# The first input loads of a fused residual + norm kernel split into small fp32 tiles

## The chip, the core and the metric

The kernel runs on one core of a Trainium2 chip. The core has five engines with a queue of instructions each: TensorE (PE, with its weight loads shown as PEld), VectorE (DVE), ScalarE (ACT), GpSimd (POOL) and SyncE (SP), and 16 DMA engines that they share. Every engine takes its instructions in order. The metric is the device time of one execution in microseconds (us), less is better.

## What is computed

```python
B, S, D = 4, 256, 256
x       = randn(B, S, D)          # float32, 1024 rows of 256
w_block = randn(D, D) * 0.05      # float32
gamma   = abs(randn(D)) + 0.5     # float32

h = maximum(x @ w_block, 0.0)
y = x + h
mu = y.mean(-1, keepdims=True)
sigma = sqrt(y.var(-1, keepdims=True) + 1e-6)
out = ((y - mu) / sigma * gamma).astype(float32)
```

The matmul is small (1024 x 256 by 256 x 256); x and the output are 1 MB each in HBM, w is 256 KB.

## The kernel before

The 1024 rows are cut into two halves (h = 0, 1) of 128 partitions x 4 rows (f), so a partition holds 4 consecutive rows of x. Each half is loaded by one DMA from POOL's queue that casts fp32 to bf16 on the way (L74); the tiles are called `x_sb_97` and `x_sb_99` in the trace. The weights w and gamma are loaded as fp32 from ACT's queue (L56, L61) and cast to bf16 on ACT (w, L58) and on DVE (gamma, L63). POOL also builds the identity matrix for the transposes (masks.py:197, a memset, and masks.py:199, an affine select).

The work then runs over four pairs of rows, `pr` = 0 to 3, each 128 partitions x 2 rows x 256:

1. PE transposes the pair in four 128x128 pieces into PSUM (L84), ACT copies them to SBUF (`xt_sb`, L89).
2. PE multiplies: four matmuls, two per row, that add up over the two halves of D (`ph`, L94).
3. ACT takes the relu out of PSUM (`relu_h`, L103). DVE adds x (`y`, L106), takes mean and variance per row (bn_stats L113, bn_aggr L114), ACT the square root (`std`, L117), DVE the reciprocal (`rstd`, L119), and DVE subtracts the mean and multiplies (`tq`, L123, two per pair).
4. POOL multiplies by gamma and writes fp32 (`o`, L133), SP issues the store (L137).

Square root needs another function table than the first copies, so ACT loads a table (ACT_TABLE_LOAD) ahead of its first `std`.

A scheduler (the Tile framework) sets the order of the instructions on each engine at build time and puts in the semaphore waits. The order in the program text is its starting point, not what stands on the engines.

Of the kernel before, what the change touches and what calls it, by code (L numbers as in the profile page):

```python
# [1 line left out]

# [15 lines left out]
def kernel(
    ctx: ExitStack,  # L20
    tc: tile.TileContext,
    x: bass.AP,
    w_block: bass.AP,
    gamma: bass.AP,
    out: bass.AP,
):
    nc = tc.nc
    P = 128

    x_flat = x.flatten_outer_dims()  # L30
    out_flat = out.flatten_outer_dims()
    N, D = x_flat.shape
    assert D == 256 and N == 1024
    KC = D // P
    G = 4
    NH = N // (P * G)
    PAIR = 2
    n_pairs = N // (P * PAIR)
# [24 lines left out]
    nc.vector.tensor_copy(out=gamma_sb, in_=gamma_stage)  # L63

    eps_sb = const.tile([P, 1], FP32)
    nc.vector.memset(eps_sb, eps)

    ident = const.tile([P, P], BF16)
    make_identity(nc, ident)

    x_sb = []
    for h in range(NH):
        t_ = xp.tile([P, G, D], BF16, name=f"x_sb{h}", tag=f"x{h}")
        nc.gpsimd.dma_start(out=t_, in_=x_v[h])  # L74
        x_sb.append(t_)

    for pr in range(n_pairs):
        h = (pr * PAIR) // G
        f0 = (pr * PAIR) % G

        pxt = ps_xt.tile([P, PAIR, KC, P], BF16)
        for t in range(PAIR):
            for c in range(KC):
                nc.tensor.transpose(  # L84
                    pxt[:, t, c, :], x_sb[h][:, f0 + t, ts(c, P)], ident
                )

        xt_sb = xtp.tile([P, PAIR, KC, P], BF16)
        nc.scalar.copy(out=xt_sb, in_=pxt)  # L89

        ph = ps_h.tile([P, PAIR, D], FP32)
        for t in range(PAIR):
# [23 lines left out]
        std = stat.tile([P, PAIR], FP32)
        nc.scalar.activation(out=std, in_=mv[:, :, 1], func=AF.Sqrt, bias=eps_sb)  # L117
        rstd = stat.tile([P, PAIR], FP32)
        nc.vector.reciprocal(out=rstd, in_=std)  # L119

        tq = op_.tile([P, PAIR, D], BF16)
        for t in range(PAIR):
# [9 lines left out]
        o = op_.tile([P, PAIR, D], FP32, tag="out")
        nc.gpsimd.tensor_tensor(  # L133
            out=o, in0=tq, in1=gamma_sb.to_broadcast([P, PAIR, D]), op=ALU.mult
        )
# [32 lines left out]
```

## Time and profile before

| | us |
|---|---|
| median of 6 runs | 26.32 (26.08 to 26.65) |
| the profiled execution's own time | 26.32 |
| its span (first to last instruction) | 24.5 |

| engine | busy us (share of the span) |
|---|---|
| DVE | 9.4 (38%) |
| ACT | 8.5 (34%) |
| POOL | 6.6 (27%) |
| PE | 5.5 (22%) |

No engine is busy for half of the span, so the sum of busy time tells little. What counts is the chain of work that ends last, followed back from the end: it holds DVE for 26% of the span, DMA for 24% (the load of `x_sb_97`), ACT for 15% and PE for 10%. The profile's other views used below are the timeline of each engine, the waits, the DMA queues, and the windows, which give the busy time in chosen stretches.

### The profile page before, as it was taken

How to read it: one execution, taken by the hardware profiler on the slowest of the kernel's cores; microseconds unless marked ns; L12 is line 12 of the kernel's file. 1: busy time of each engine (PE TensorE's matmuls, PEld its weight loads, DVE VectorE, ACT ScalarE, POOL GpSimd, SP SyncE). 2: the span in 40 equal slices, each digit the busy share in tenths (PEclk: the TensorE clock that was granted, in tenths of full speed). 3: DMA queues.
4: the chain of work that ended last, by engine and by line, in shares of the span. 5: the costliest groups of instructions: out<-in, count | busy, mean ns of one | idle time of the engine just before them, and what ended most of it. 6: DMA issues, size and time to landing. Idle time of an engine off the chain costs nothing.

```text
span 24.5 us, 182 instructions
## 1 busy us (share of the span) xinstructions
PE 5.5 (22%) x32; PEld 3.8 (15%) x32; DVE 9.4 (38%) x34; ACT 8.5 (34%) x15; POOL 6.6 (27%) x12
## 2 busy tenths in 40 slices
PE   0000000000039599994994000000000000000000
PEld 0000000000038277772770000000000000000000
DVE  0000000004000000599930999999998991000000
ACT  0029836000003945599999990000242000000000
POOL 3398600000000000000000049509802966920000
PEclk9999999999999999999999999975555555555555
DMA  0009727699973000000000000009107400913700
GB/s 0 0 7 245 264 32 72 122 160 204 197 137 57 0 0 0 0 0 0 0 0 0 0 0 0 0 0 377 50 0 280 147 0 0 381 47 127 301 0 0
DMA packets 1280, 1.97 MB, mean 80 GB/s; under 512 B 128, under 2 KB 512, under 8 KB 1280
## 3 DMA queue, kind: packets, MB, share of 16 engines
q0 software_dynamic: 288, 0.52, 13.0%
q1 hardware_dynamic: 576, 1.05, 11.4%
q10 hardware_dynamic: 416, 0.39, 5.6%
HBM read 1.44 MB, written 1.05 MB: 101 GB/s over the span
## 4 chain that ended last, share of the span: by engine, by line
DVE 26%; DMA 24%; ACT 15%; PE 10%; issue 5%; POOLq 5%; POOL 1%; DVEq 0%
DMA x_sb_97<-in_x_dram 24%; DVE tq L123 11%; PE ph L94 8%; ACT xt_sb L89 6%; DVE y L106 6%; ACT L117 5%; POOLq L163 5%; DVE bn_181 L113 3%; PE pxt L84 3%; DVE bn_213 L113 3%; ACT relu_h L103 2%; DVE rstd L119 2%; DVE mv L114 2%; ACT std L117 1%; POOL ident masks.py:197 1%
## 5 line engine op out<-in xcount | busy, mean ns | idle before, releaser
L133 POOL TENSOR_TENSOR o<-tq,gamma_sb 128x512 f32<-128x512 bf16 x4 | 4.7, 1173 | 14.1 <-DVE tq L123 12.5
L94 PE MATMUL ph<-w_sb,xt_sb 128*128 128x256 bf16 x16 | 3.6, 402 | 0.6 <-ACT xt_sb L89 0.6
L89 ACT COPY xt_sb<-pxt 128x512 bf16<-128x512 bf16 x4 | 2.1, 590 | 3.7 <-PE pxt L84 3.7
L123 DVE TENSOR_SCALAR tq<-y,mv,rstd 128x256 bf16<-128x256 bf16 x8 | 3.1, 434 | 0.1
L84 PE MATMUL pxt<-ident,x_sb_97 128*128 128x128 bf16 x8 | 1.0, 311 | 7.1 <-DMA x_sb_97<-in_x_dram 7.1
L103 ACT ACTIVATE relu_h<-ph 128x512 bf16<-128x512 f32 x4 | 2.3, 590 | 0.9 <-PE ph L94 0.9
L106 DVE TENSOR_TENSOR y<-x_sb_97,relu_h 128x512 bf16<-128x512 bf16 x2 | 0.8, 409 | 4.1 <-ACT relu_h L103 4.1
L94 PEld LDWEIGHTS <-xt_sb 128*128 128x128 bf16 x16 | 2.1, 140 | 1.8 <-ACT xt_sb L89 1.1
L117 ACT ACTIVATE std<-mv,eps_sb 128x2 f32<-128x2 f32 x4 | 1.2, 295 | 3.3 <-DVE mv L114 3.3
L63 DVE CAST gamma_sb<-gamma_stage 128x256 bf16<-128x256 f32 x1 | 0.3, 294 | 4.9 <-DMA gamma_stage<-in_gamma_dram 4.9
L58 ACT ACT_TABLE_LOAD x1 | 1.3, 1283 | 1.7 <-PEq L152 1.7
L84 PEld LDWEIGHTS <-x_sb_97 128*128 128x128 bf16 x8 | 0.8, 140 | 7.1 <-DMA x_sb_97<-in_x_dram 7.1
L106 DVE TENSOR_TENSOR y<-x_sb_99,relu_h 128x512 bf16<-128x512 bf16 x2 | 1.6, 802 | 0.0
L117 ACT ACT_TABLE_LOAD x1 | 1.3, 1283 | 0.0
L84 PE MATMUL pxt<-ident,x_sb_99 128*128 128x128 bf16 x8 | 1.1, 314 | 0.0
L119 DVE RECIPROCAL rstd<-std 128x2 f32<-128x2 f32 x4 | 0.7, 164 | 1.1 <-ACT std L117 1.0
L84 PEld LDWEIGHTS <-x_sb_99 128*128 128x128 bf16 x8 | 0.9, 151 | 0.1
L74 POOL DMA_DIRECT2D x_sb_97<-in_x_dram x1 | 0.7, 714 | 0.3 <-issue 0.3
L58 ACT CAST w_sb<-w_stage 128x512 bf16<-128x512 f32 x1 | 0.6, 617 | 0.5 <-DMA w_stage<-in_w_block_dram 0.5
L113 DVE BATCH_NORM_STATS2 bn_213<-y 128x6 f32<-128x256 bf16 x2 | 0.8, 384 | 0.0
L113 DVE BATCH_NORM_STATS2 bn_117<-y 128x6 f32<-128x256 bf16 x2 | 0.8, 418 | 0.0
L113 DVE BATCH_NORM_STATS2 bn_149<-y 128x6 f32<-128x256 bf16 x2 | 0.8, 418 | 0.0
(13 smaller groups left out, 3.5 us busy)
## 6 DMA issues: line engine op xcount, KB each, us to landing
out_dram<-o SPq DMA_DIRECT2D x4, 256.0 KB, 2.0
w_stage<-in_w_block_dram ACTq DMA_DIRECT2D x1, 256.0 KB, 2.7
x_sb_97<-in_x_dram POOLq DMA_DIRECT2D x1, 256.0 KB, 5.8
x_sb_99<-in_x_dram POOLq DMA_DIRECT2D x1, 256.0 KB, 6.0
gamma_stage<-in_gamma_dram ACTq DMA_DIRECT2D x1, 128.0 KB, 4.5
```

The source lines that it names most:

```text
L58: nc.scalar.copy(out=w_sb, in_=w_stage)
L84: nc.tensor.transpose(pxt[:, t, c, :], x_sb[h][:, f0 + t, ts(c, P)], ident)
L89: nc.scalar.copy(out=xt_sb, in_=pxt)
L94: nc.tensor.matmul(ph[:, t, :], lhsT=xt_sb[:, t, c, :], rhs=w_sb[:, c, :], start=(c == 0), stop=(c == KC - 1),)
L103: nc.scalar.activation(out=relu_h, in_=ph, func=AF.Relu)
L106: nc.vector.tensor_tensor(out=y, in0=x_sb[h][:, f0 : f0 + PAIR, :], in1=relu_h, op=ALU.add)
L113: nc.vector.bn_stats(out=bn6[:, t, :], in_=y[:, t, :])
L117: nc.scalar.activation(out=std, in_=mv[:, :, 1], func=AF.Sqrt, bias=eps_sb)
L119: nc.vector.reciprocal(out=rstd, in_=std)
L123: nc.vector.tensor_scalar(tq[:, t, :], in0=y[:, t, :], scalar1=mv[:, t, 0:1], scalar2=rstd[:, t : t + 1], op0=ALU.subtract, op1=ALU.mult,)
L133: nc.gpsimd.tensor_tensor(out=o, in0=tq, in1=gamma_sb.to_broadcast([P, PAIR, D]), op=ALU.mult)
L163: with _tile.TileContext(nc) as tc:
```

## The change

- Of the first half of x, the first two rows per partition come as two tiles of 128 x 256 in **fp32**, `x_t0` and `x_t1`, loaded without a cast by SP. The other two rows are a bf16 tile `x_p1` (128 x 512) and the second half is a bf16 tile `x_p23` (128 x 1024); both are loaded with the cast by POOL, as before.
- w and gamma move from ACT's queue to SP's, behind the two x tiles; the cast of w moves from ACT to DVE.
- There are two identities, fp32 and bf16, both built ahead of POOL's loads.
- The work runs over five units in place of four pairs: u0 and u1 of one row per partition, u2, u3 and u4 of two. The transposes of u0 and u1 are in fp32.
- For u4 the multiplication by gamma moves from POOL to DVE, with a bf16 result `ob`, and its store moves to POOL's queue, which casts bf16 to fp32 on the way out.
- The pool of `y` has 4 buffers in place of 3; x tiles have one each.

```diff
+    ident_f32 = const.tile([P, P], FP32)
+    make_identity(nc, ident_f32)
+    ident = const.tile([P, P], BF16)
+    make_identity(nc, ident)
+
+    x_t0 = xp.tile([P, 1, D], FP32, name="x_t0", tag="x_t0")
+    nc.sync.dma_start(out=x_t0, in_=x_v[0][:, 0:1, :])
+    x_t1 = xp.tile([P, 1, D], FP32, name="x_t1", tag="x_t1")
+    nc.sync.dma_start(out=x_t1, in_=x_v[0][:, 1:2, :])
     w_stage = const.tile([P, KC, D], FP32)
-    nc.scalar.dma_start(out=w_stage, in_=w_block.rearrange("(kc p) n -> p kc n", p=P))
+    nc.sync.dma_start(out=w_stage, in_=w_block.rearrange("(kc p) n -> p kc n", p=P))
+    gamma_stage = const.tile([P, 1, D], FP32)
+    nc.sync.dma_start(out=gamma_stage, in_=gamma.partition_broadcast(P))
+    x_p1 = xp.tile([P, 2, D], BF16, name="x_p1", tag="x_p1")
+    nc.gpsimd.dma_start(out=x_p1, in_=x_v[0][:, 2:4, :])
+    x_p23 = xp.tile([P, G, D], BF16, name="x_p23", tag="x_p23")
+    nc.gpsimd.dma_start(out=x_p23, in_=x_v[1])
+
     w_sb = const.tile([P, KC, D], BF16)
-    nc.scalar.copy(out=w_sb, in_=w_stage)
+    nc.vector.tensor_copy(out=w_sb, in_=w_stage)
...
-    x_sb = []
-    for h in range(NH):
-        t_ = xp.tile([P, G, D], BF16, name=f"x_sb{h}", tag=f"x{h}")
-        nc.gpsimd.dma_start(out=t_, in_=x_v[h])
-        x_sb.append(t_)
+        idm = ident_f32 if x_dt == FP32 else ident
+        pxt = ps_xt.tile([P, 2, KC, P], x_dt, tag=f"pxt_{x_dt}")
+        for t in range(nt):
+            for c in range(KC):
+                nc.tensor.transpose(pxt[:, t, c, :], xs[:, t, ts(c, P)], idm)
...
+        if apply2_eng == "gp":
+            o = op_.tile([P, 2, D], FP32, tag="out_f32")
+            nc.gpsimd.tensor_tensor(
...
+            nc.sync.dma_start(out=out_v[h][:, f0 : f0 + nt, :], in_=o[:, 0:nt])
+        else:
+            ob = op_.tile([P, 2, D], BF16, tag="out_bf16")
+            nc.vector.tensor_tensor(
...
+            nc.gpsimd.dma_start(out=out_v[h][:, f0 : f0 + nt, :], in_=ob[:, 0:nt])
 
-        nc.sync.dma_start(out=out_v[h][:, f0 : f0 + PAIR, :], in_=o)
+    process_unit(x_t0, 0, 0, 1, "gp", "u0")
+    process_unit(x_t1, 0, 1, 1, "gp", "u1")
+    process_unit(x_p1, 0, 2, 2, "gp", "u2")
+    process_unit(x_p23[:, 0:2, :], 1, 0, 2, "gp", "u3")
+    process_unit(x_p23[:, 2:4, :], 1, 2, 2, "ve", "u4")
```

Three places show what the scheduler makes of it. On PE, at the start of the changed kernel (`x_t_92` and `x_t_94` are the fp32 tiles x_t0 and x_t1, `x_p_100` is x_p1, `x_p_102` is x_p23; the matmuls on `xt_sb` are first the two of u0, then the two of u1):

```order
L84 MATMUL pxt<-ident_f_82,x_t_92 128x128 x2
L84 MATMUL pxt<-ident_f_82,x_t_94 128x128 x2
L84 LDWEIGHTS x_p_100
L84 MATMUL pxt<-ident,x_p_100 128x128
L92 LDWEIGHTS xt_sb
L92 MATMUL ph<-w_sb,xt_sb 128x256
L92 LDWEIGHTS xt_sb
L92 MATMUL ph<-w_sb,xt_sb 128x256
```

The first transpose of u2, with its weight load from `x_p_100`, stands ahead of the first matmul of u0.

On ACT, the whole of the changed kernel's queue up to its end (128x256 are u0 and u1, the first two 128x512 copies are u2 and u3):

```order
L87 ACT_TABLE_LOAD
L87 CAST xt_sb<-pxt 128x256 x2
L101 ACTIVATE relu_h<-ph 128x256 x2
L87 COPY xt_sb<-pxt 128x512 x2
L101 ACTIVATE relu_h<-ph 128x512
L115 ACT_TABLE_LOAD
L115 ACTIVATE std<-mv,eps_sb 128x1 x2
L101 ACTIVATE relu_h<-ph 128x512
L87 COPY xt_sb<-pxt 128x512
L101 ACTIVATE relu_h<-ph 128x512
L115 ACTIVATE std<-mv,eps_sb 128x2 x3
```

The square roots of u0 and u1 stand behind the copies of u2 and u3, the relu of u2 and the table load.

On POOL, from the identities on, the changed kernel has:

```order
masks.py:197 MEMSET ident_f_82 128x128
masks.py:197 MEMSET ident 128x128
masks.py:199 ISA
masks.py:199 AFFINE_SELECT ident_f_82<-ident_f_82 128x128
masks.py:199 AFFINE_SELECT ident<-ident 128x128
L66 DMA x_p_100<-in_x_dram 128x512
L68 DMA x_p_102<-in_x_dram 128x1024
L134 TENSOR_TENSOR o<-tq,gamma_sb 128x256 x2
L134 TENSOR_TENSOR o<-tq,gamma_sb 128x512 x2
L149 DMA out_dram<-ob 128x512
```

Two memsets and two selects stand ahead of the first load, where before it was one memset, and the last store is now at the end of this queue.

## Rows read from the trace of the kernel before

**Rows 1.** The chain that ended last: start us, us, what.
```profile
1.25 5.83 DMA x_sb_97<-in_x_dram
...
11.92 1.28 ACT L117
13.21 0.30 ACT std L117
...
20.45 1.18 POOLq L163
```

**Rows 2.** The waits: total us, times, longest us.
```profile
PE pxt L84 <- DMA x_sb_97<-in_x_dram: 7.1, 1, 7.1
```

**Rows 3.** The timeline of POOL at the start: start us, us, instruction.
```profile
0.74 0.20 POOL masks.py:197 MEMSET ident<- 128x128 bf16 x1 [0.29 <-POOLq L152]
1.25 0.71 POOL L74 DMA_DIRECT2D x_sb_97<-in_x_dram  x1 [0.31 <-issue]
2.06 0.30 POOL masks.py:199 TENSOR_SCALAR_AFFINE_SELECT ident<-ident 128x128 bf16<-128x128 bf16 x1
2.30 0.56 POOL L74 DMA_DIRECT2D x_sb_99<-in_x_dram  x1
```

**Rows 4.** The timeline of ACT and DVE: the load of w, the cast of gamma.
```profile
0.74 0.42 ACTq L56 DMA_DIRECT2D w_stage<-in_w_block_dram  x1
...
5.76 0.29 DVE L63 CAST gamma_sb<-gamma_stage 128x256 bf16<-128x256 f32 x1 [4.89 <-DMA gamma_stage<-in_gamma_dram]
```

**Rows 5.** DMA issues: queue, count, KB each, median us from issue to landing.
```profile
out_dram<-o SPq DMA_DIRECT2D x4, 256.0 KB, 2.0
w_stage<-in_w_block_dram ACTq DMA_DIRECT2D x1, 256.0 KB, 2.7
x_sb_97<-in_x_dram POOLq DMA_DIRECT2D x1, 256.0 KB, 5.8
x_sb_99<-in_x_dram POOLq DMA_DIRECT2D x1, 256.0 KB, 6.0
gamma_stage<-in_gamma_dram ACTq DMA_DIRECT2D x1, 128.0 KB, 4.5
```

**Rows 6.** DMA queues, 3.4 to 3.7 us: packets, MB, share of 16 engines.
```profile
q0 software_dynamic: 1, 0.00, 17.0%
```

**Rows 7.** DMA queues, 5.0 to 5.5 us (q10: w and gamma).
```profile
q10 hardware_dynamic: 7, 0.00, 6.0%
```

**Rows 8.** DMA queues, 5.5 to 6.0 us (q0: POOL's loads of x).
```profile
q0 software_dynamic: 56, 0.11, 113.5%
```

**Rows 9.** Windows: stretch, its length, busy per engine, clock, DMA share, GB/s.
```profile
23.20:23.50 0.30, 0.00 (x0) 0.00 (x0) 0.00 (x0) 0.00 (x0) 0.00 (x0) 0.50 0.03 7
```

**Rows 10.** Timeline of PE: start us, us for the group, instruction.
```profile
7.12 1.03 PE L84 MATMUL pxt<-ident,x_sb_97 128*128 128x128 bf16 x8 [7.12 <-DMA x_sb_97<-in_x_dram]
8.41 1.89 PE L94 MATMUL ph<-w_sb,xt_sb 128*128 128x256 bf16 x8 [0.25 <-ACT xt_sb L89]
```

**Rows 11.** Groups of instructions: count, busy us, mean ns, idle before.
```profile
L103 ACT ACTIVATE relu_h<-ph 128x512 bf16<-128x512 f32 x4 | 2.3, 590 | 0.9 <-PE ph L94 0.9
L106 DVE TENSOR_TENSOR y<-x_sb_97,relu_h 128x512 bf16<-128x512 bf16 x2 | 0.8, 409 | 4.1 <-ACT relu_h L103 4.1
L119 DVE RECIPROCAL rstd<-std 128x2 f32<-128x2 f32 x4 | 0.7, 164 | 1.1 <-ACT std L117 1.0
```

**Rows 12.** Timeline of DVE and POOL, from 13.7 us on.
```profile
13.77 0.58 DVE L123 TENSOR_SCALAR tq<-y,mv,rstd 128x256 bf16<-128x256 bf16 x2
16.40 0.74 DVE L113 BATCH_NORM_STATS2 bn_181<-y 128x6 f32<-128x256 bf16 x2
17.06 0.16 DVE L114 BATCH_NORM_AGGREGATE mv<-bn_181 128x2 f32<-128x6 f32 x1
18.85 1.15 POOL L133 TENSOR_TENSOR o<-tq,gamma_sb 128x512 f32<-128x512 bf16 x1 [1.15 <-DVE rstd L119]
18.96 1.38 DVE L123 TENSOR_SCALAR tq<-y,mv,rstd 128x256 bf16<-128x256 bf16 x2
```

More of the change, by code (lines that the diff above doesn't have):

```diff
@@ L35 @@
     G = 4
-    NH = N // (P * G)
-    PAIR = 2
-    n_pairs = N // (P * PAIR)
     eps = 1e-6
@@ L45 @@
     const = ctx.enter_context(tc.tile_pool(name="const", bufs=1))
-    xp = ctx.enter_context(tc.tile_pool(name="xp", bufs=2))
+    xp = ctx.enter_context(tc.tile_pool(name="xp", bufs=1))
     xtp = ctx.enter_context(tc.tile_pool(name="xtp", bufs=3))
     hp = ctx.enter_context(tc.tile_pool(name="hp", bufs=3))
-    yp = ctx.enter_context(tc.tile_pool(name="yp", bufs=3))
+    yp = ctx.enter_context(tc.tile_pool(name="yp", bufs=4))
     op_ = ctx.enter_context(tc.tile_pool(name="op", bufs=3))
@@ L53 @@
     ps_h = ctx.enter_context(tc.tile_pool(name="ps_h", bufs=4, space=bass.MemoryType.PSUM))
-    w_stage = const.tile([P, KC, D], FP32)
-    nc.scalar.dma_start(out=w_stage, in_=w_block.rearrange("(kc p) n -> p kc n", p=P))
+    ident_f32 = const.tile([P, P], FP32)
[6 more added lines that the diff above has]
+    nc.sync.dma_start(out=x_t1, in_=x_v[0][:, 1:2, :])
+    w_stage = const.tile([P, KC, D], FP32)
+    nc.sync.dma_start(out=w_stage, in_=w_block.rearrange("(kc p) n -> p kc n", p=P))
[5 more added lines that the diff above has]
+    nc.gpsimd.dma_start(out=x_p23, in_=x_v[1])
     w_sb = const.tile([P, KC, D], BF16)
-    nc.scalar.copy(out=w_sb, in_=w_stage)
-    gamma_stage = const.tile([P, 1, D], FP32)
-    nc.scalar.dma_start(out=gamma_stage, in_=gamma.partition_broadcast(P))
+    nc.vector.tensor_copy(out=w_sb, in_=w_stage)
     gamma_sb = const.tile([P, 1, D], BF16)
@@ L66, with process_unit @@
     nc.vector.memset(eps_sb, eps)
-    ident = const.tile([P, P], BF16)
-    make_identity(nc, ident)
-    x_sb = []
-    for h in range(NH):
-        t_ = xp.tile([P, G, D], BF16, name=f"x_sb{h}", tag=f"x{h}")
-        nc.gpsimd.dma_start(out=t_, in_=x_v[h])
-        x_sb.append(t_)
[L77 to L82, printed above, removed]
-            for c in range(KC):
[L84 to L92, printed above, removed]
+    def process_unit(xs, h, f0, nt, apply2_eng, tagsfx):
+        x_dt = xs.dtype
+        idm = ident_f32 if x_dt == FP32 else ident
+        pxt = ps_xt.tile([P, 2, KC, P], x_dt, tag=f"pxt_{x_dt}")
+        for t in range(nt):
+            for c in range(KC):
+                nc.tensor.transpose(pxt[:, t, c, :], xs[:, t, ts(c, P)], idm)
+        xt_sb = xtp.tile([P, 2, KC, P], BF16)
+        nc.scalar.copy(out=xt_sb[:, 0:nt], in_=pxt[:, 0:nt])
+        ph = ps_h.tile([P, 2, D], FP32)
+        for t in range(nt):
             for c in range(KC):
@@ L100 @@
                 )
-        relu_h = hp.tile([P, PAIR, D], BF16)
-        nc.scalar.activation(out=relu_h, in_=ph, func=AF.Relu)
-        y = yp.tile([P, PAIR, D], BF16)
+        relu_h = hp.tile([P, 2, D], BF16)
+        nc.scalar.activation(out=relu_h[:, 0:nt], in_=ph[:, 0:nt], func=AF.Relu)
+        y = yp.tile([P, 2, D], BF16)
         nc.vector.tensor_tensor(
-            out=y, in0=x_sb[h][:, f0 : f0 + PAIR, :], in1=relu_h, op=ALU.add
+            out=y[:, 0:nt], in0=xs[:, 0:nt], in1=relu_h[:, 0:nt], op=ALU.add
         )
-        bn6 = stat.tile([P, PAIR, 6], FP32)
-        mv = stat.tile([P, PAIR, 2], FP32)
-        for t in range(PAIR):
+        bn6 = stat.tile([P, 2, 6], FP32)
+        mv = stat.tile([P, 2, 2], FP32)
+        for t in range(nt):
             nc.vector.bn_stats(out=bn6[:, t, :], in_=y[:, t, :])
             nc.vector.bn_aggr(out=mv[:, t, :], in_=bn6[:, t, :])
[L116 to L122, printed above, removed]
+        std = stat.tile([P, 2], FP32)
+        nc.scalar.activation(
+            out=std[:, 0:nt], in_=mv[:, 0:nt, 1], func=AF.Sqrt, bias=eps_sb
+        )
+        rstd = stat.tile([P, 2], FP32)
+        nc.vector.reciprocal(out=rstd[:, 0:nt], in_=std[:, 0:nt])
+        tq = op_.tile([P, 2, D], BF16)
+        for t in range(nt):
             nc.vector.tensor_scalar(
@@ L130 @@
             )
[L132 to L135, printed above, removed]
-        nc.sync.dma_start(out=out_v[h][:, f0 : f0 + PAIR, :], in_=o)
+        if apply2_eng == "gp":
+            o = op_.tile([P, 2, D], FP32, tag="out_f32")
+            nc.gpsimd.tensor_tensor(
+                out=o[:, 0:nt],
+                in0=tq[:, 0:nt],
+                in1=gamma_sb.to_broadcast([P, nt, D]),
+                op=ALU.mult,
+            )
+            nc.sync.dma_start(out=out_v[h][:, f0 : f0 + nt, :], in_=o[:, 0:nt])
+        else:
+            ob = op_.tile([P, 2, D], BF16, tag="out_bf16")
+            nc.vector.tensor_tensor(
+                out=ob[:, 0:nt],
+                in0=tq[:, 0:nt],
+                in1=gamma_sb.to_broadcast([P, nt, D]),
+                op=ALU.mult,
+            )
+            nc.gpsimd.dma_start(out=out_v[h][:, f0 : f0 + nt, :], in_=ob[:, 0:nt])
[4 more added lines that the diff above has]
+    process_unit(x_p23[:, 2:4, :], 1, 2, 2, "ve", "u4")
 _INS = ['x', 'w_block', 'gamma']
```

## Prediction, made before the changed kernel ran

> **What bounds the kernel now.** I read the chain of waits first, then the waits, then the timelines. The chain opens with the cast load of the first half of x: issued by POOL at 1.25, landed 5.83 later [rows 1], and until then PE stands idle for 7.1 us, its one long wait [rows 2]. From there one thread runs through transposes, copies, matmuls and relu, ACT's table load (11.92 to 13.20) and the first square root [rows 1], then DVE without a gap, then POOL's last multiplication by gamma (20.45 to about 21.65) and the last store, 2.0 from issue to landing [rows 1, 5]. The windows show that the store's data are through at about 23.2 [rows 9], so its landing is about 21.7 + 2.0 = 23.7; the span ends at 24.5, 0.8 after it. The profiled execution took 26.32 with a span of 24.5, so 1.8 lie outside the span; 26.32 is also the median. All sums below are spans, with 1.8 added at the end.
>
> So three stretches can shrink: the 7.1 at the start, the middle from the landing to DVE's end (7.1 to 20.3), and the 4.2 from DVE's end to the end.
>
> **The change, part by part.**
>
> *When the new first tiles land.* SP issues x_t0 at about 0.74, where ACT issued w [rows 4]. It has 128 KB and no cast; 256 KB took 2.0 for a store and 2.7 for w [rows 5], so it lands at 2.7 to 3.5, and x_t1 one issue (0.42) [rows 4] later. w is issued third, at about 0.74 + 2 x 0.42 = 1.6, and lands at 4.3, or 0.5 later if it shares the engines; its cast on DVE is bounded by twice the 0.29 of gamma's, which is half its size [rows 4], so w_sb is there by 5.4. The fp32 transposes have no row. A bf16 one takes 1.03 / 8 = 0.13 in a stream of eight [rows 10], which bounds it from below; four of them fit between 3.5 and the landing of x_p1 (6.3, below) even at 0.7 each, so I cost them at nothing; that cover is gone if one takes over 0.7. The same holds for ACT's two casts.
>
> *What that buys: nothing directly.* PE's order has the first transpose of u2 ahead of the first matmul of u0. PE takes its queue in order, so every matmul waits for x_p1, a cast load by POOL like the one that PE waits for today. The early tiles only shorten what comes behind that load.
>
> *When x_p1 lands.* Before, the first load was issued at 1.25. Now a second memset (0.20) and two selects (0.30 each) stand ahead of it [rows 3]: 1.25 + 0.8 = 2.05, and x_p23 0.75 later, at 2.8. From issue to landing there are two bounds. From above the old 5.8 [rows 5]: 7.85. From below, the queue without disturbance: 0.71 of issue [rows 3], 0.9 to the end of a first packet (an estimate, half of the 1.7 between the issue's end, 1.96, and the first packet of this queue, which ended by 3.7 [rows 6], behind w), 8 packets per engine of half the bytes at half of 16 x 0.5 x 1.135 / 56 = 0.16 [rows 8], 0.65, and 0.5 from the last data to the landing, as at the store's end (23.2 to 23.7): 2.8, so 4.85. In between: x's queue reaches its full rate only as gamma's packets end, at about 5.5 [rows 7, 8], and gamma is now issued 0.8 later, behind more bytes, so it is again in the way; but x_p1's packets are half as long, which takes 0.65 off the upper bound. I take 6.3, the middle of 4.85 and 7.85, which is 0.8 earlier than today. x_p23 has 8 whole packets more per engine, 8 x 0.16 = 1.3, so about 7.7.
>
> *From x_p1 to the table load.* PE: one transpose, the four matmuls of u0 and u1, three transposes, that is half of eight transposes (0.52) and half of eight matmuls (0.95) [rows 10]: 7.8. ACT's relus of u0 and u1 lie beside that. The copy of u2, 0.59 as the relu [rows 11]: 8.4; of u3, to 9.0, beside the four matmuls of u2 (again 0.95, and 0.1 for handovers): 9.45. The relu of u2: 10.05. This stretch does not wait for x_p23 as long as that lands by about 8.1; at 8.6 it costs 0.5. Then the table load, 1.28 [rows 1]: 11.35, where the old one ended at 13.20. So 1.85 is gained here: 0.8 from the landing and the rest because the table load no longer stands behind four copies.
>
> *From the table load to DVE's end.* Two square roots (u0, u1) and the relu of u3, each starting a little before the one ahead of it ends, to 12.35, the copy of u4 to 12.85, its matmuls 1.05, its relu: 14.5, and beside its end the square root of u2, 0.30 [rows 1], to 14.7. DVE has u0's and u1's work and the y of u3 done by then. Reciprocal 0.16 [rows 11], aggregates 0.16, two tq, 0.58 [rows 12]: 15.6. Here POOL starts u2's multiplication, 1.15, and a tq issued meanwhile ends only after it: the pair at 18.96 took 1.38 in place of 0.58 [rows 12]. So u3's tq end at 15.6 + 1.15 + 0.55 = 17.3 (the y of u4 is inside). Then u4: statistics 0.74, aggregates 0.16, square root 0.30, reciprocal 0.16, tq 0.58 and the handovers between them: 19.3, and the new multiplication on DVE, priced as the y of the same size, 0.41 [rows 11]: 19.7. Before, DVE ended at 18.96 + 1.38 = 20.34 [rows 12] and POOL at about 21.65.
>
> A wait that is added: the casts of w and gamma stand at the head of DVE's queue, ahead of every y. gamma, issued fourth at about 2.0, lands near 2.0 + 4.5 = 6.5 [rows 5]; the first y is due at 7.5 and DVE has slack up to 10. It is hidden.
>
> *The last store.* It was issued by SP and landed in 2.0 [rows 5]; now POOL issues it, with a cast. The only rows of that queue are loads: 5.8 and 6.0 [rows 5], the upper bound. The lower is the plain store, 2.0, plus POOL's longer issue, 0.71 in place of about 0.35: 2.4. I build it as above: 0.71 + 0.9 + 8 x 0.16 + 0.5 = 3.4 (taking its packets as long as the loads'), since nothing else is on the DMA engines then, and take that. The page "DMA: Bandwidth & Descriptors" of the Trainium skill (Anatomy of one DMA, SWDGE path) has a rule for this queue: about 2.0 us fixed plus the bytes at 436 GB/s, an estimate of 2.6 us for 256 KB. The loads of this trace took 5.8 to 6.0, so as it stands the rule does not hold at the start of this kernel; no row shows the queue alone.
>
> *The sum.* 19.7 + 3.4 + 0.8 = 23.9 against 24.5; with 1.8, **25.7 us**, 2.4% less.
>
> **The rivals.**
>
> *Faster still: the POOL queue is quick when it is alone.* The store costs its lower bound, 2.4 to 2.6, or x_p1 lands by 5.4. For it: no row shows this queue undisturbed. Against it: one packet of this queue had ended by 3.7, 2.4 after the issue [rows 6]. Either gives 0.8 to 0.9 less: 24.8 us. By the page's rule it would be the same 24.9.
>
> *No change: x_p1 lands when x_sb_97 did.* The queue's latency is a matter of starting 16 engines and not of bytes, and gamma's packets are still about. Landing at 7.1 puts 0.8 on everything: 24.7 + 1.8 = 26.5 us.
>
> *Slower: the last store on POOL's queue eats the gain.* The store ends the kernel and nothing covers it. The break-even is 24.5 - 0.8 - 19.7 = 4.0 us from issue to landing, with x_p1 at 6.3; with x_p1 at 7.1 it is 3.2. At the loads' 5.8 the span is 26.3, so 28.1 us; at 4.8, 27.1. For it: both rows of this queue are at or above 5.8, and each of their packets passes through a cast, as the store's do. Against it: those loads shared the engines with w, gamma and each other, which the store does not.
>
> **How the numbers follow.** Forecast 0.38 (25.2 to 26.05); faster still 0.17; no change 0.17; slower 0.28, most of it at stores of 4.2 to 5 us. One per cent, about what a measurement of this kernel can tell from no change, is 0.26, so faster is below 26.06: 0.38 + 0.17 = 0.55; same 0.17; slower 0.28. The range reaches into the faster rival (24.8) a little beyond its value and into the slower one up to a store of about 5.2: 24.6 to 27.5; outside it I leave 0.07 below and 0.12 above. The forecast's own range is 25.2 to 26.05.
>
> **What would show it.** The profile of the changed kernel should show PE's transposes of x_t0 at about 3, then PE idle until x_p1 lands, at about 6.3, and its first matmul right after that and not before. ACT's second table load should start at about 10. DVE's last instruction should be the multiplication by gamma, at about 19.3, and POOL's store 3.4 from issue to landing. The forecast is wrong if the landing of x_p1 is not what releases the first matmul, if x_p23 is later than 8.1, or if the store takes 4 or more; and the part on fp32 is wrong if the transposes are still running when x_p1 is there.

## The result

| | changed | before |
|---|---|---|
| median, us | 25.74 (25.28 to 26.42, 10 runs) | 26.36 (26.06 to 26.69, 20 runs) |
| the profiled execution's own time | 26.03 | 26.32 |
| its span | 24.3 | 24.5 |
| its landing of the first cast load | 6.7 | 7.1 |
| its last `tq` ends | 20.0 | 20.3 |

The changed kernel is **faster**: ratio 0.970, 95% interval 0.964 to 0.976; the forecast was 25.7 us, 2.4% less than 26.32. The ratio compares the quickest runs of both kernels, and the profiled execution is one of the changed kernel's slower ones, so its profile shows where the time lies, and sums are made against its own 24.3 and 26.03. That execution is 0.29 below the one before (26.03 against 26.32), while the medians are 0.62 apart (0.977 as a ratio); where the other 0.3 lies no trace shows.

### The profile page after: what moved, and what is told of

Its sections match the earlier page's. It is cut to its first block, busy times and chain, and to the rows that moved or that the text cites. A ratio compares the mean times of both kernels' runs of the same rounds, so it can differ in the third digit from the quotient of the medians.

```text
span 24.3 us, 202 instructions
## 1 busy us (share of the span) xinstructions
PE 6.7 (28%) x32; PEld 3.9 (16%) x32; DVE 10.3 (42%) x38; ACT 8.6 (35%) x17; POOL 6.8 (28%) x15
## 3 DMA queue, kind: packets, MB, share of 16 engines
q1 hardware_dynamic: 1280, 1.44, 17.3%
HBM read 1.44 MB, written 1.05 MB: 103 GB/s over the span
## 4 chain that ended last, share of the span: by engine, by line
DMA 21%; ACT 17%; issue 16%; PE 13%; DVE 8%; POOL 8%; POOLq 3%; ACTq 0%
DMA x_p_100<-in_x_dram 21%; PE ph L92 12%; ACT relu_h L101 8%; DVE tq L123 7%; POOL o L134 5%; ACT xt_sb L87 4%; ACT std L115 3%; POOLq L181 3%; ACT L115 1%; PE pxt L84 1%; POOL ident_f_82 masks.py:199 1%; DVE rstd L119 1%; POOL ident masks.py:197 1%; POOL ident masks.py:199 1%; DVE mv L112 1%
## 5 line engine op out<-in xcount | busy, mean ns | idle before, releaser
L134 POOL TENSOR_TENSOR o<-tq,gamma_sb 128x256 f32<-128x256 bf16 (+1 forms) x4 | 4.0, 1002 | 12.3 <-DVE tq L123 10.4
L101 ACT ACTIVATE relu_h<-ph 128x512 bf16<-128x512 f32 (+1 forms) x5 | 2.5, 507 | 4.0 <-PE ph L92 4.0
L115 ACT ACTIVATE std<-mv,eps_sb 128x2 f32<-128x2 f32 (+1 forms) x5 | 1.4, 290 | 3.3 <-DVE mv L112 3.3
L119 DVE RECIPROCAL rstd<-std 128x2 f32<-128x2 f32 (+1 forms) x5 | 0.8, 163 | 2.0 <-ACT std L115 1.9
L87 ACT CAST xt_sb<-pxt 128x256 bf16<-128x256 f32 x2 | 0.7, 372 | 2.4 <-PE pxt L84 2.4
L84 PE MATMUL pxt<-ident_f_82,x_t_92 128*128 128x128 f32 x2 | 0.7, 434 | 3.3 <-DMA x_t_92<-in_x_dram 3.3
L149 POOL DMA_DIRECT2D out_dram<-ob x1 | 0.6, 599 | 1.6 <-DVE ob L143 1.6
L104 DVE TENSOR_TENSOR y<-x_p_102,relu_h 128x512 bf16<-128x512 bf16 x2 | 0.9, 446 | 0.0
L104 DVE TENSOR_TENSOR y<-x_p_100,relu_h 128x512 bf16<-128x512 bf16 x1 | 0.4, 426 | 0.9 <-ACT relu_h L101 0.9
L111 DVE BATCH_NORM_STATS2 bn_176<-y 128x6 f32<-128x256 bf16 x2 | 0.8, 400 | 0.0
```

The lines of the kernel that those rows point to most:

```text
L84: nc.tensor.transpose(pxt[:, t, c, :], xs[:, t, ts(c, P)], idm)
L87: nc.scalar.copy(out=xt_sb[:, 0:nt], in_=pxt[:, 0:nt])
L101: nc.scalar.activation(out=relu_h[:, 0:nt], in_=ph[:, 0:nt], func=AF.Relu)
L104: nc.vector.tensor_tensor(out=y[:, 0:nt], in0=xs[:, 0:nt], in1=relu_h[:, 0:nt], op=ALU.add)
L115: nc.scalar.activation(out=std[:, 0:nt], in_=mv[:, 0:nt, 1], func=AF.Sqrt, bias=eps_sb)
L119: nc.vector.reciprocal(out=rstd[:, 0:nt], in_=std[:, 0:nt])
```

## The profile after

The chain that ended last in the changed kernel (start us, us, what) answers to [rows 1]:

```profile
1.60 5.08 DMA x_p_100<-in_x_dram
6.68 0.04 issue
6.73 0.29 PE pxt L84
7.02 0.87 PE ph L92 x4
...
10.56 0.36 ACT L115
10.92 0.94 issue
11.85 0.48 ACT std L115 x2
...
16.40 1.10 DVE tq L123
17.50 0.47 issue
17.97 1.15 POOL o L134
19.12 1.63 issue
20.75 0.62 POOLq L181
```

The chain still opens with a cast load by POOL, now of half the size. It then has the same links as before: PE, ACT's table load, DVE, POOL. Two of its "issue" pieces are work or a wait: the 0.94 at 10.92 is the rest of the table load (1.28 from 10.56), and in the 1.63 at 19.12 POOL waits for DVE's `ob`, which ends at 20.47.

PE of the changed kernel (start us, us for the group, instruction; the idle time ahead of it and its releaser in brackets) answers to [rows 2, 10]:

```profile
3.28 0.66 PE L84 MATMUL pxt<-ident_f_82,x_t_92 128*128 128x128 f32 x2 [3.28 <-DMA x_t_92<-in_x_dram]
4.07 0.69 PE L84 MATMUL pxt<-ident_f_82,x_t_94 128*128 128x128 f32 x2
6.73 0.29 PE L84 MATMUL pxt<-ident,x_p_100 128*128 128x128 bf16 x1 [1.97 <-DMA x_p_100<-in_x_dram]
6.81 1.06 PE L92 MATMUL ph<-w_sb,xt_sb 128*128 128x256 bf16 x4
```

PE starts at 3.28 in place of 7.12, is through with the fp32 transposes by 4.8, and stands idle until `x_p_100` lands. The first matmul comes 0.08 behind that transpose. The early start buys nothing directly.

The DMA issues (KB each, us from issue to landing) answer to [rows 5]:

```profile
x_t_92<-in_x_dram SPq DMA_DIRECT2D x1, 128.0 KB, 2.4
w_stage<-in_w_block_dram SPq DMA_DIRECT2D x1, 256.0 KB, 4.2
gamma_stage<-in_gamma_dram SPq DMA_DIRECT2D x1, 128.0 KB, 4.8
x_p_100<-in_x_dram POOLq DMA_DIRECT2D x1, 128.0 KB, 5.1
x_p_102<-in_x_dram POOLq DMA_DIRECT2D x1, 256.0 KB, 5.8
out_dram<-ob POOLq DMA_DIRECT2D x1, 256.0 KB, 2.3
```

Half the bytes bring the cast load down only from 5.8 to 5.1 in these two executions. The last store on POOL's queue takes 2.3, against 2.0 by SP before.

Windows of both kernels (stretch, its length, busy us of PE, PEld, DVE, ACT, POOL, granted clock, DMA share, GB/s): from the gate, the first transpose that waits for a cast load, to the first square root, and from there to the end of the last `tq`. Before:

```profile
7.12:13.21 6.09, 5.46 (x32) 3.78 (x32) 2.36 (x8) 4.52 (x7) 0.00 (x0) 1.00 0.05 10
13.21:20.34 7.13, 0.00 (x0) 0.00 (x0) 6.67 (x24) 2.04 (x6) 3.54 (x3) 0.71 0.20 74
```

After:

```profile
6.73:11.85 5.12, 4.34 (x24) 2.84 (x24) 2.45 (x8) 3.76 (x6) 0.00 (x0) 1.00 0.13 24
11.85:20.01 8.16, 1.03 (x4) 0.43 (x4) 6.94 (x27) 2.81 (x8) 3.98 (x4) 1.00 0.19 66
```

The first stretch is 0.97 shorter, since the table load no longer stands behind four copies of 128x512; the second is 1.03 longer. DVE was idle for 0.46 of it before (7.13 - 6.67) and is idle for 1.22 now, and works 0.27 more. From the gate to the last `tq` both take 13.2 to 13.3.

## The experiments

Each is timed against the kernel before on the same chip; the rows come from several chips, so ratios are compared and not times.

| run | edit | median, us | ratio to before (interval) |
|---|---|---|---|
| changed kernel | | 25.74 | 0.970 (0.964 to 0.976) |
| a_end_undone | last unit by POOL and SP again | 26.04 | 0.965 (0.960 to 0.971) |
| b_end_only | before + last pair's new end | 26.61 | 1.005 (1.002 to 1.007) |
| c_gamma_plain | gamma's load made a plain one of rows of w (gamma's values left out) | 25.24 | 0.952 (0.948 to 0.955) |
| f_w_on_act | w and gamma on ACT's queue | 25.74 | 0.969 (0.966 to 0.973) |
| k_ungated | PE order: u0, u1 not behind u2 | 25.65 | 0.970 (of the medians, no interval; the changed kernel's is 0.977) |
| g_bf16_front | no fp32 tiles | 25.00 | 0.945 (0.939 to 0.951) |
| h_table_first | square root's table first | 24.25 | 0.910 (0.904 to 0.917) |
| i_before_table | before + that table first | 25.31 | 0.957 (0.952 to 0.963) |
| j_bf16_table | g + that table first | 23.80 | 0.885 (0.880 to 0.890) |
| e_front_all | all of the first half fp32 by SP, and more | 22.17 | 0.841 (0.836 to 0.845) |
| n_front_u3 | e + u3 ends as u4 does | 21.68 | 0.810 (0.804 to 0.816) |
| l_bf16_all | n without fp32 tiles | 23.13 | 0.867 (0.861 to 0.873) |

### Does the end gain or cost? (a_end_undone, b_end_only)

In the first, the last unit of the changed kernel goes back to POOL and SP; in the second, the kernel before gets the new end alone.

```diff
-    process_unit(x_p23[:, 2:4, :], 1, 2, 2, "ve", "u4")
+    process_unit(x_p23[:, 2:4, :], 1, 2, 2, "gp", "u4")
```

```diff
-        o = op_.tile([P, PAIR, D], FP32, tag="out")
-        nc.gpsimd.tensor_tensor(
-            out=o, in0=tq, in1=gamma_sb.to_broadcast([P, PAIR, D]), op=ALU.mult
-        )
-        nc.sync.dma_start(out=out_v[h][:, f0 : f0 + PAIR, :], in_=o)
+        if pr < n_pairs - 1:
...
+        else:
+            ob = op_.tile([P, PAIR, D], BF16, tag="out_bf16")
+            nc.vector.tensor_tensor(
+                out=ob, in0=tq, in1=gamma_sb.to_broadcast([P, PAIR, D]), op=ALU.mult
+            )
+            nc.gpsimd.dma_start(out=out_v[h][:, f0 : f0 + PAIR, :], in_=ob)
```

> The changed kernel with u4's gamma multiplication back on POOL and its store back on SP; the order on PE, ACT and DVE is otherwise the same. In the changed kernel the last tq ends at about 20.0 and the span at 24.3. Theory (the gain is in the front: x_p1's landing and the table load standing earlier; the new end only breaks even): tq at 20.0, POOL 1.15, issue, 2.0 to landing, about 1.0 to the end, span 24.2 to 24.3, time as the changed kernel within 1%, about 3% faster than before. Rival (the gain is the new end, POOL's multiplication no longer stands behind DVE): span about 25.0, time as before or slower, 0.99 to 1.02 of before.

> The kernel before with the last pair's gamma multiplication on DVE (bf16) and its store on POOL's queue, nothing else. Theory (the new end breaks even): DVE's last tq at 20.3, multiplication 0.43, 0.3 to the issue, 2.3 to landing, 1.2 to the end: span 24.5 to 24.6, ratio 0.99 to 1.01 of before. Rival (the new end is the gain): ratio 0.96 to 0.98.

Undoing the end moves nothing that the intervals can tell (0.965 against 0.970); the end alone gives 1.005. In the trace of b_end_only the last `tq` of DVE, the multiplication, and the store on POOL (start us, us):

```profile
19.12 1.39 DVE L123 TENSOR_SCALAR tq<-y,mv,rstd 128x256 bf16<-128x256 bf16 x2
20.55 0.43 DVE L140 TENSOR_TENSOR ob<-tq,gamma_sb 128x512 bf16<-128x512 bf16 x1
```
```profile
21.27 0.60 POOL L143 DMA_DIRECT2D out_dram<-ob  x1 [1.10 <-DVE ob L140]
```

The `tq` ends at 20.51 and the span at 24.8, so the end takes 4.29; with POOL and SP it took 24.5 - 20.34 = 4.16 in the kernel before. DVE's 0.43 in place of POOL's 1.15 saves 0.72; it goes to 0.29 between `ob` and the issue, to 0.4 more from issue to landing (2.4 against 2.0 [rows 5]), and to some 1.1 behind the landing (21.27 + 2.4 = 23.67 to 24.8) in place of 0.8. The end breaks even, or costs half a per cent: the whole gain is at the front.

### What gates the front? (c_gamma_plain, f_w_on_act, k_ungated)

```diff
-    nc.sync.dma_start(out=gamma_stage, in_=gamma.partition_broadcast(P))
+    nc.sync.dma_start(out=gamma_stage, in_=w_block[0:P, :].unsqueeze(1))
```

> The changed kernel with the gamma load (one 1 KB row read 128 times) replaced by a plain load of the same size, 128 different rows of w; gamma's values are therefore left out of the result. Theory (gamma's slow packets hold up x_p1 and w on the DMA engines): gamma lands in 2.5 to 3 in place of 4.8, w in about 3, x_p1 in 4.2 to 4.6 in place of 5.1, span 23.5 to 23.8, ratio 0.94 to 0.96 of before. Rival (POOL's queue takes about 5 us at the start of the kernel whatever else is in flight): x_p1 at 5.0 to 5.2, time as the changed kernel.

```diff
-    nc.sync.dma_start(out=w_stage, in_=w_block.rearrange("(kc p) n -> p kc n", p=P))
+    nc.scalar.dma_start(out=w_stage, in_=w_block.rearrange("(kc p) n -> p kc n", p=P))
     gamma_stage = const.tile([P, 1, D], FP32)
-    nc.sync.dma_start(out=gamma_stage, in_=gamma.partition_broadcast(P))
+    nc.scalar.dma_start(out=gamma_stage, in_=gamma.partition_broadcast(P))
```

> The changed kernel with the loads of w and gamma issued from ACT's queue as before, w at about 0.74 in place of 1.64; the rest as it was. Theory (the first matmul is released by x_p1, which stands ahead of it on PE): w's cast ends by 4.5, yet the first matmul starts with x_p1, at 6.5 to 6.7, time within 1% of the changed kernel. Rival (w is the gate: its cast ended at 6.27, 0.5 before the first matmul): first matmul by 5.5, span about 1 us shorter, ratio 0.93 to 0.95 of before.

In k_ungated only the order on PE changes: u2's transposes are issued behind u1's last matmul.

```diff
+        with tc.issue_after(last_mm["u1"].ins) if tagsfx == "u2" else nullcontext():
+            for t in range(nt):
...
-                nc.tensor.matmul(
+                last_mm[tagsfx] = nc.tensor.matmul(
```

> The changed kernel with one ordering constraint: u2's transposes stand behind u1's last matmul on PE; every other engine's order is as changed, the second table load too. Theory (the gate is released, but the next one stands close behind it: PE's transposes of x_p23 stand ahead of u2's matmuls, and the table load behind u2's relu): first matmul at 5.0 to 6.3 with w's cast, table load only 0.3 to 0.6 earlier, span 23.6 to 24.0, 1 to 2% less than the changed kernel. Rival (the gate alone holds everything): the table load follows the 1.5 of the first matmul, span 22.8 or less, ratio 0.93 or less of before. Second rival (the gate costs nothing): time within 0.5% of the changed kernel.

With gamma's broadcast gone about 2% of the time went (0.952 against 0.970), so gamma's packets cost something. By which load they do the one trace doesn't show: `x_p1` took 4.8, where 4.2 to 4.6 was expected, and `x_p23` 5.3, in place of 5.1 and 5.8, but the same loads differ by more than that between executions. In the four profiled ones that issue the changed kernel's loads at the same times (the changed kernel, a, h, k) `x_p1` took 5.1, 5.5, 4.5 and 5.7 and `x_p23` 5.4 to 6.2. The lines of a, h and k:

```profile
x_p<-in_x_dram POOLq DMA_DIRECT2D x1, 128.0 KB, 5.5
```
```profile
x_p<-in_x_dram POOLq DMA_DIRECT2D x1, 128.0 KB, 4.5
```
```profile
x_p<-in_x_dram POOLq DMA_DIRECT2D x1, 128.0 KB, 5.7
```

So a difference of a few tenths between two landings shows nothing. Most of the 5.1 remains in c. With w on ACT's queue its cast was done at 4.90, well before `x_p1` landed, and the first matmul still waited (6.67, behind a transpose at 6.60): w is not the gate, and the time did not move. PE of k_ungated:

```profile
5.57 1.01 PE L95 MATMUL ph<-w_sb,xt_sb 128*128 128x256 bf16 x4 [0.96 <-DVE w_sb L71]
7.32 0.61 PE L87 MATMUL pxt<-ident,x_p 128*128 128x128 bf16 x4 [0.74 <-DMA x_p<-in_x_dram]
8.50 0.61 PE L87 MATMUL pxt<-ident,x_p 128*128 128x128 bf16 x4 [0.58 <-DMA x_p<-in_x_dram]
8.90 1.06 PE L95 MATMUL ph<-w_sb,xt_sb 128*128 128x256 bf16 x4
```

The matmuls of u0 and u1 start 1.24 earlier, at 5.57, released by the cast of w. But u2's matmuls stand behind the transposes that need `x_p23`, at 8.90 against 8.87 in the changed kernel, and the table load comes at 10.62 against 10.56. So the gate is real, and the next cast load is a second gate behind it. What taking the first away is worth by itself these runs tell only roughly: in this execution both cast loads landed later than in the changed kernel's (7.3 and 8.5 against 6.7 and 8.1), so the two places of the table load can't be compared as they stand, and by medians the run is at 0.970 against 0.977. The 1 to 2% that was expected is not shown.

### Do the fp32 tiles pay? (g_bf16_front)

All of x comes by POOL in bf16; u0 and u1 use a third cast load.

```diff
-    x_t0 = xp.tile([P, 1, D], FP32, name="x_t0", tag="x_t0")
-    nc.sync.dma_start(out=x_t0, in_=x_v[0][:, 0:1, :])
-    x_t1 = xp.tile([P, 1, D], FP32, name="x_t1", tag="x_t1")
-    nc.sync.dma_start(out=x_t1, in_=x_v[0][:, 1:2, :])
+    x_p0 = xp.tile([P, 2, D], BF16, name="x_p0", tag="x_p0")
+    nc.gpsimd.dma_start(out=x_p0, in_=x_v[0][:, 0:2, :])
...
-    process_unit(x_t0, 0, 0, 1, "gp", "u0")
-    process_unit(x_t1, 0, 1, 1, "gp", "u1")
+    process_unit(x_p0[:, 0:1, :], 0, 0, 1, "gp", "u0")
+    process_unit(x_p0[:, 1:2, :], 0, 1, 1, "gp", "u1")
```

> The changed kernel without its fp32 tiles: u0 and u1 take their rows from one bf16 tile that POOL loads with the cast, ahead of x_p1 and x_p23; units, w, gamma and the end as changed. Theory (the early fp32 tiles buy nothing by themselves, since the first matmul waits for a POOL load of half the old size in both kernels): the first load lands at 6.4 to 6.8, its matmuls start by 8, time within 1.5% of the changed kernel, ratio 0.96 to 0.985 of before. Rival (the fp32 tiles are the gain): ratio 0.99 to 1.01 of before.

This was the surprise: without the tiles that give the change its name the kernel is faster than with them, 0.945 against 0.970, and below the range that was expected. Its DMA issues:

```profile
w_stage<-in_w_block_dram SPq DMA_DIRECT2D x1, 256.0 KB, 3.0
x_p<-in_x_dram POOLq DMA_DIRECT2D x2, 128.0 KB, 4.1
gamma_stage<-in_gamma_dram SPq DMA_DIRECT2D x1, 128.0 KB, 3.6
```

Without the two fp32 tiles the cast loads of 128 KB took 4.1 (in j too), against 4.5 to 5.7 in the four executions with them, and gamma 3.6 (3.7 in j) against 4.4 to 5.3: by about 1 us quicker than in the changed kernel, and quicker than in any of the four. For w nothing is shown: 3.0 here, 3.0 to 4.2 there. In g w and gamma are also issued earlier, at 0.74 and 1.22; but f issues them at these times with the tiles about, and `x_p1` took 4.9 and gamma 4.4, so some 0.8 of it goes with the tiles (one execution each). At the gate that is worth little between these two executions: the first cast load is through at 5.75, but its transposes and copy, 0.86, which the fp32 tiles had hidden, now lie behind it, and the first matmul runs at 6.61 in place of 6.81. The larger difference between them comes by way of ACT's order, which the scheduler made anew:

```profile
8.10 1.07 ACT L85 COPY xt_sb<-pxt 128x512 bf16<-128x512 bf16 x2
9.19 1.28 ACT L113 ACT_TABLE_LOAD   x1
10.49 0.30 ACT L113 ACTIVATE std<-mv,eps_sb 128x1 f32<-128x1 f32 x1
10.69 0.58 ACT L99 ACTIVATE relu_h<-ph 128x512 bf16<-128x512 f32 x1
```

The table load stands ahead of u2's relu here and behind it in the changed kernel, so it starts at 9.19 in place of 10.56, and DVE's last `tq` ends at 18.96 in place of 20.01. How much of the gain is the tiles' and how much this order's, g alone doesn't tell; j, with no table load in the middle, does so below. What is plain is that the early fp32 data are not what the change gains by. What g keeps of the change gains more without them: the cut of the first cast load into halves, u0 and u1 as small units, w and gamma by SP, the cast of w on DVE, and the end, which breaks even. Which of these brings the gain no run separates.

### What else stands in the middle? (h_table_first, i_before_table, j_bf16_table)

One call asks ACT for a square root of `eps_sb` before any other work of ACT's, in the changed kernel (h), in the kernel before (i), and in g_bf16_front (j).

```diff
     nc.vector.memset(eps_sb, eps)
+    sq0 = const.tile([P, 1], FP32)
+    nc.scalar.activation(out=sq0, in_=eps_sb, func=AF.Sqrt)
```

> The changed kernel with one square root of eps on ACT at the start, so that the first table load brings the table of the square root and no second one stands in the middle; the scheduler then also puts u0's and u1's matmuls ahead of x_p1's transposes on PE. Theory (table load and gate lie on the path): first matmul at w's cast, 5.2 to 6.3, before x_p1 lands; no DVE idle of 1.2 ahead of the first reciprocal; last tq at about 18.7, span 22.8 to 23.3, ratio 0.92 to 0.94 of before. Rival (DVE held up by POOL's multiplications sets the end whatever comes before): last tq at 19.7 or later, time within 1% of the changed kernel.

> The kernel before with the same square root of eps at the start and nothing else: it takes the second table load (1.28, 11.92 to 13.20) off the path. Theory: the idle of 1.04 on DVE ahead of the first reciprocal goes, span 23.4 to 23.7, ratio 0.955 to 0.97 of before, that is as much as the whole change brought. Rival (the table load is hidden, DVE has other work): ratio 0.99 to 1.01.

> No fp32 tiles (u0 and u1 from a bf16 tile that POOL loads first) and the square root table first: beside the run that had the fp32 tiles and the table first, this shows what the fp32 tiles are worth once PE may start on them. Theory (the fp32 tiles still delay POOL's loads by about 1 us, and the later units set the end): first matmul at about 6.6 in place of 5.3, yet x_p23 lands as early or earlier, time 0.90 to 0.925 of before, within 1.5% of that run. Rival (an early start is worth its 1.3 us once the gate is gone): 0.94 or more of before.

ACT of i_before_table has one table load in the whole kernel, where there were two:

```profile
1.71 1.28 ACT L68 ACT_TABLE_LOAD   x1 [1.71 <-PEq L154]
...
11.14 1.07 ACT L91 COPY xt_sb<-pxt 128x512 bf16<-128x512 bf16 x2
12.15 0.30 ACT L119 ACTIVATE std<-mv,eps_sb 128x2 f32<-128x2 f32 x1
```

The table of the square root serves the copies and the relu as well, so 1.28 goes from the path that ends last: 4.3% for one call in the old kernel, more than the whole change gives. The page "ScalarE: Activation LUTs" of the Trainium skill (Table sets) says that relu and copy are in every set and to group calls by set; the trace agrees: after one load the three kinds run without another. In h the call also moves the scheduler: PE has u2's transposes behind u1's matmuls there, so with the gate of `x_p1` gone at the same time (first matmul at 5.32) it gives 6 points, more than the expected range (0.92 to 0.94). h is therefore not the table alone; i is. The same call in g (j, 0.885, expected 0.90 to 0.925) keeps g's lead over the fp32 kernel with it (h, 0.910), where the place of the table load plays no part any more: by these times the two fp32 tiles are dear with PE's gate and without it. The traces don't show where: the profiled execution of j took 24.38 against a median of 23.80, and its first matmul, at 6.46, and its last `tq`, ended at 18.28, are behind h's 5.32 and 17.95.

### When do fp32 tiles pay? (e_front_all, n_front_u3, l_bf16_all)

e takes the causes found together: the rest of the first half in fp32 by SP too, w on ACT's queue, gamma cast by POOL behind `x_p23`, and the table first. n adds u3's end on DVE; l is n with all of x by POOL in bf16 (the edit of g).

```diff
+    x_p1 = xp.tile([P, 2, D], FP32, name="x_p1", tag="x_p1")
+    nc.sync.dma_start(out=x_p1, in_=x_v[0][:, 2:4, :])
-    nc.sync.dma_start(out=w_stage, in_=w_block.rearrange("(kc p) n -> p kc n", p=P))
-    gamma_stage = const.tile([P, 1, D], FP32)
-    nc.sync.dma_start(out=gamma_stage, in_=gamma.partition_broadcast(P))
-    x_p1 = xp.tile([P, 2, D], BF16, name="x_p1", tag="x_p1")
-    nc.gpsimd.dma_start(out=x_p1, in_=x_v[0][:, 2:4, :])
+    nc.scalar.dma_start(out=w_stage, in_=w_block.rearrange("(kc p) n -> p kc n", p=P))
...
+    gamma_sb = const.tile([P, 1, D], BF16)
+    nc.gpsimd.dma_start(out=gamma_sb, in_=gamma.partition_broadcast(P))
```

> A version that follows the findings: the changed kernel with x_p1 in fp32 by SP too, w from ACT's queue at the start, gamma loaded with a cast by POOL behind x_p23 (no slow packets ahead of x, no cast on DVE), and the square root table first. Theory: first matmul at 4.5 to 5.2, x_p23 lands at 6.3 to 6.8 and is the last gate, last tq at 16.5 to 17.2, span 20.8 to 21.6, ratio 0.86 to 0.89 of before. Rival (fp32 transposes of x_p1 and DVE's blocked operations eat it): span 22.5 or more, ratio 0.91 or more.

```diff
-    process_unit(x_p23[:, 0:2, :], 1, 0, 2, "gp", "u3")
+    process_unit(x_p23[:, 0:2, :], 1, 0, 2, "ve", "u3")
```

> The version that followed the findings (x_p1 in fp32 by SP, w from ACT's queue, gamma by POOL behind x_p23, table first) with u3's gamma multiplication on DVE and its store on POOL's queue too. Theory (u4's tq waited 0.85 for POOL's multiplication of u3, DVE pays 0.43 for doing it): last tq 0.4 earlier, span 19.9 to 20.2, ratio 0.82 to 0.835. Rival (two stores on POOL's queue get in each other's way): ratio 0.84 or more.

> The version of n_front_u3 with all of x loaded by POOL with the cast to bf16 and no fp32 tile (x_p0 for u0 and u1, x_p1, x_p23, then gamma, all on POOL's queue; w from ACT's). SP loads nothing. Theory (the fp32 tiles are dear even where everything else is mended): in g_bf16_front the first POOL load landed 4.1 after its issue and the first matmul ran at 6.6; here nothing but w loads beside it, so 3.8 to 4.1, transposes at 5.4 to 5.7, first matmul at about 6.1, but x_p1 and x_p23 close behind and all y of 128x512 in bf16 (0.42 in place of 0.69); ratio 0.80 to 0.82, no worse than n_front_u3. Rival (fp32 by the hardware queue pays once nothing stands behind it): n_front_u3's first matmul ran at 5.2 and its DVE went from 9.5 on without idle time; a start one microsecond later moves everything: ratio 0.83 to 0.86.

PE of n_front_u3, the best version:

```profile
5.21 0.63 PE L92 MATMUL ph<-w_sb,xt_sb 128*128 128x256 bf16 x2
5.64 0.42 PE L84 MATMUL pxt<-ident_f,x_p 128*128 128x128 f32 x1
...
6.92 1.06 PE L84 MATMUL pxt<-ident,x_p 128*128 128x128 bf16 x8
7.81 1.89 PE L92 MATMUL ph<-w_sb,xt_sb 128*128 128x256 bf16 x8
```

and of l_bf16_all:

```profile
6.08 1.03 PE L90 MATMUL ph<-w_sb,xt_sb 128*128 128x256 bf16 x4 [0.25 <-ACT xt_sb L85]
6.91 0.63 PE L82 MATMUL pxt<-ident,x_p 128*128 128x128 bf16 x4
7.88 0.61 PE L82 MATMUL pxt<-ident,x_p 128*128 128x128 bf16 x4 [0.33 <-DMA x_p<-in_x_dram]
```

e and n came out below their expected ranges. Here the answer turns round, and the expectation for l (no worse than n) fell: with fp32 0.810, without 0.867. In n only one cast load of x is left, for u3 and u4; it was issued at 1.63 and its transposes run at 6.92, at once behind u2's, while in l it is the third on POOL's queue and lands at 7.8. From the first matmul on PE has no idle time in n up to 9.70, and DVE (the third column of busy time) works through from 9.51 to its end:

```profile
9.51:16.02 6.51, 0.80 (x5) 0.31 (x4) 6.43 (x26) 2.43 (x6) 2.95 (x3) 0.78 0.23 81
```

The last `tq` of l ends 1.37 later than n's (16.93 against 15.56). Of that 0.87 is there at the first matmul (6.08 against 5.21), and u3's `tq` took 1.19 beside POOL's multiplication of u2, where n's took 0.60; this hangs on when POOL's work falls, so not all of the difference is the loads'. A version with all of x in bf16 and fewer cast loads was not run.

n is 21.68 us, 16% below the changed kernel's median. It is bound by DVE from 9.5 to 16.0 and by the last store.

## Why the prediction was right

The forecast, 25.7, and its gate held: the cast load `x_p1` releases the first matmul, it lands a little earlier than the old one in the profiled execution, and little of the kernel's time goes. The split of the gain did not hold. The forecast had the last `tq` 1.0 earlier (19.3 against 20.34) and an end that costs 0.45 (0.4 + 3.4 + 0.8 = 4.6 against 4.16); the profiled execution has 0.33 (20.01) and 0.13 (4.29), and b_end_only has the end at 0.5%. So the sum is near because errors of both signs cancel, and that it met the median to 0.04 is luck. In spans, predicted 23.9 and measured 24.3 in the profiled execution:

| step | predicted | measured | adds |
|---|---|---|---|
| POOL issues `x_p1` | 2.05 | 1.60 | -0.45 |
| from issue to landing | 4.25 | 5.08 | +0.83 |
| from landing to the table load | 3.75 | 3.88 | +0.13 |
| from there to `ob`'s end | 9.65 | 9.91 | +0.26 |
| from there to the store's issue | 0 | 0.30 | +0.30 |
| from issue to landing of the store | 3.4 | 2.3 | -1.10 |
| from landing to the end | 0.8 | 1.23 | +0.43 |

- **The gate held.** The first matmul waits for `x_p1` behind one transpose; k_ungated shows the wait by taking it away, and f_w_on_act that it is not w. Harmless, but off: w landed at 5.84, a microsecond and more behind the 4.3 to 4.8 predicted, and its cast ended at 6.27, 0.5 ahead of the gate where 0.9 was forecast. The fp32 transposes stayed under their bound (0.66 to 0.69 for two, 0.7 for each was allowed), and `x_p23` landed at 2.27 + 5.8 = 8.1, just at the bound named for it: u2's matmuls follow ACT's copy, not it.
- **The issue of `x_p1` was mis-sized.** I added a memset and two selects end to end to the old 1.25. They overlap: memsets at 0.74 and 0.88, selects at 1.12 and 1.37, and the 0.31 that POOL waited before its first load [rows 3] is inside that.
- **Its latency was mis-sized the other way.** I took 6.3 as the middle between the old 5.8 from issue to landing and a queue without disturbance, with gamma as the thing in the way. (The middle of 4.85 and 7.85 is 6.35, and the 0.65 for shorter packets, which I take off the upper bound there, is not in it; with it the middle is 6.0, farther off.) All four executions with these loads are above the 4.25 that this leaves, 4.5 to 5.7. The two fp32 tiles are in the way too: with them gone it is 4.1 (g). The early tiles, which I costed at nothing, cost some 0.8 to 1 us in the landing of the first cast load, and give 0.86 back by the transposes and the copy that they hide.
- **The middle.** The table load came at 10.56 against 10.05, as the landing moved (0.38) and 0.13 more. That it starts 1.36 earlier than in the old kernel is given back on DVE behind it, which the windows above show and the step of 9.65 had nearly in full: 0.33 of it is left at the last `tq`.
- **The store was mis-sized, to the good.** It took 2.3; I built 3.4 out of packets as slow as the loads'. The page "DMA: Bandwidth & Descriptors" of the Trainium skill (Anatomy of one DMA, SWDGE path) gives an estimate of 2.6, and is nearer. At the start of the kernel, with other loads about, 128 KB took 3.6 to 5.7 on the same queue in these runs, against an estimate by that rule of 2.3. The rival that the store eats the gain (break-even 4.0) fell with it: b_end_only is 1.005 and not 1.07.
- **"Faster still" did not come** although its condition, a store of 2.4 to 2.6, was met: the late landing of `x_p1` and 0.73 of handover and tail around the store that I had not counted took it back. "No change" fell too, but not by much: 6.7 lies midway between 7.1 and the 6.3 I took, and in a and k, with the same loads, `x_p1` landed at 7.1 and 7.3, when the old load did (7.1 to 7.4 in the kernel before, b and i).

## What to carry to other kernels

An early load is worth what the instruction that waits last gains: before splitting one, look in each engine's order for what stands ahead of the early work, and count what the new transfers add to the latency of those that remain. Splitting paid here only when the whole of the gate went to the quick path (n against l); half of it there and half on the slow path was worse than both halves on the slow path (g). Look at ACT's table loads first: one call that loads the square root's table at the start was worth more than this whole change. And before reading a few tenths between two landings, look how far the same load moves between executions; here it was 1.2 us.

## What the runs showed of the hardware

- **The same loads do not land alike.** With the loads issued within 0.05 us of the same times, the first cast load took 4.5 to 5.7 in four executions, w 3.0 to 4.2 and gamma 4.4 to 5.3. The landing is where the chain starts, and 1.2 is as much as the changed kernel's runs scatter (25.28 to 26.42); that the one makes the other is not shown.
- **Loads issued early slow those behind them.** Two plain tiles of 128 KB on SP's queue add some 0.8 to the landing of gamma and of the first cast load (4.4 and 4.9 in f, 3.6 and 4.1 in g, with w and gamma issued at the same times), on loads from two queues. The page "DMA: Bandwidth & Descriptors" of the Trainium skill (Issuing engines are not separate DMA queues) says that all queues run on the same 16 engines and interleave, which fits.
- **A `tq` on DVE waits out a multiplication on POOL**: the pair at 16.40 of the changed kernel took 1.43 while POOL's `o` ran from 16.17 to 17.49, and the pair at 19.41 took 0.60 with POOL idle. e lost 0.84 so at its end (1.44 at 14.72, `o` from 14.67); n, which takes that `o` off POOL, has 0.60 there.
- **PE's clock rows and durations do not fit together.** In the changed kernel the granted clock reads 1.00 (2.4 GHz) over the whole span, and u4's four matmuls took 1.03:

```profile
13.34 1.03 PE L92 MATMUL ph<-w_sb,xt_sb 128*128 128x256 bf16 x4 [2.16 <-ACT xt_sb L87]
```

In a_end_undone, where the row falls to 0.69 and 0.50 (1.2 GHz) behind that place, the same four took 0.61, after the same work and as long a wait:

```profile
13.78 0.61 PE L92 MATMUL ph<-w_sb,xt_sb 128*128 128x256 bf16 x4 [2.23 <-ACT xt_sb L87]
```

There the gate came 0.44 later (7.17) and the last `tq` started at the same time (19.42 against 19.41), which the 0.42 fits; two executions show no more than that. The other traces go the same way: the four took 1.03 or 1.04 in f, g, h, j and k, which read 1.00 to the end, and 0.61 to 0.95 in c, e, l and n, which do not. What the changed kernel's times scatter by is something else: its five executions that read 1.00 took 25.49 to 26.40, and its six that read 0.77 to 0.81 took 25.28 to 26.42.
